# Last batch of a cross-covariance attention with a gated feed-forward: pairs of chunks, and every second block by seven products for eight

## The chip, the core and the metric

The kernel runs on one core of a Trainium2 chip. The core has five engines with instruction queues of their own, which meet only at semaphores: TensorE (PE in the profile) multiplies matrices into PSUM, VectorE (DVE) and ScalarE (ACT) read PSUM and SBUF, GpSimd (POOL) works on SBUF alone, and SyncE (SP) issues DMAs. [...] The metric is the device time of one execution in microseconds (us); lower is better. Before the change the median of three runs is 555.26 us (555.23 to 555.40).

## The reference

Four batches of 5824 tokens with 256 channels go through an attention over channels; its output goes as tokens through a feed-forward in which two products of the same input are multiplied with each other:

```python
qn = q / (norm(q, axis=1) + 1e-06);  kn = k / (norm(k, axis=1) + 1e-06)
a = softmax(kn.transpose(0, 2, 1) @ qn / tau)       # 256 x 256 per batch
x = (v @ a).reshape(B * S, D)                       # 23296 x 256
out = ((x @ w1) * (x @ w2)) @ w3 @ w_out            # 1024 hidden, 256 out
```

## The kernel before

Nothing non-linear stands between `v @ a` and `x @ w1`, so the kernel folds: for each batch `Wf = a @ [w1, w2]` (256 x 2 x 1024, bf16, by `fold`), and once `W_sb = w3 @ w_out` (1024 x 256). Per token what is left is `((v Wf1) * (v Wf2)) W_sb`. v comes in pieces of eight token groups by POOL's DMA queue and is transposed by DMA on SP's queue, into `vT` (channels on partitions).

A batch's tokens are cut into 12 chunks: eleven of 512 and a rest of 192. The loop at the end of the kernel goes over batches, chunks and the eight blocks j of 128 hidden columns; a step of it is a slot. In a slot `emit_ab` lets PE do four 512-column products: a = Wf1 block by vT (two, for the two channel halves, summed in PSUM) and b the same way with Wf2. ACT casts a to bf16 (`as`, line 663), and DVE multiplies it with b out of PSUM into `abh` in SBUF (line 676). The four PSUM banks `ab0` to `ab3` are taken in turn.

The second product, `abh` by `W_sb`, is done for whole chunks by a scheme of seven block products where the plain way has eight (`seven_products`): four operands S1 to S4, sums and differences of quarters of `abh` (lines 589 and 592, 128x1024 bf16 with both inputs in SBUF), then seven groups of eight 128-column products (`prodA`, `prodB`, `prodC`, line 570), with copies by ACT (`keep`, line 580) and additions by DVE (`join`, line 583) into the output tile. In batches 0 to 2 S1 to S4 are made by POOL, in the last batch by DVE. The groups wait in the list `pend` and are put behind the products of later slots, at most so many per slot as `room` allows. Chunks 10 and 11 of the last batch take the plain way (`emit_out`).

The program's order is written out by hand: what is emitted first stands first in its engine's queue. An agenda (`at`, `run_due`) puts the attention of batch n + 1 into batch n's slots by a running estimate of PE's time, and the loads of q, k and v, each behind a one-element copy on POOL (`gate`, line 645) that waits for a recent `abh`. In the last batch there is no next attention: what is left are the loads of v (pieces 2 to 5) and the feed-forward. SBUF tiles of 4 KB per partition (pieces, `abh` halves) share 21 buffers of the tag `big`.

Of the kernel before, what the change touches and what calls it, by code (L numbers as in the profile page):

```python
# [25 lines left out]
def kernel(  # L26
# [250 lines left out]
    def soft_units(n):  # L277
# [199 lines left out]
        if n == 0:  # L477
# [7 lines left out]
            + [(0.0, 11 + 1.4 * ct, lambda ct=ct: exps(ct)) for ct in range(CT)]  # L485
            + [(0.2, 15, sums)]
            + [(0.43, 16.5 + 1.1 * i, lambda i=i: fold(i)) for i in range(8)]
        )


    clock = [0.0]
    agenda = []
# [59 lines left out]
    def seven_products(b, c, k1, k2):  # L552
# [6 lines left out]
        w22 = [W_sb[:, 4 + j, P:] for j in range(4)]  # L559
        t1, t2, t3, t4 = ([T[:, i, j, :] for j in range(4)] for i in range(4))  # L560
        st, sums = {}, {}
        tags = {"A": "out0", "B": "out1", "C": "out1" if b < B - 1 else "out2"}
        adder = nc.gpsimd if b < B - 1 else nc.vector

        def product(nm, a, w, first=False):
            if first:
# [63 lines left out]
        def then(fn):  # L630
            return lambda: following.append(fn)

        if b == B - 1:
            return [S(1)], [
                [S(2), p1], [S(3), p5], [p6], [S(4), p7], [J("C", 1, 1), p2],
                [J("B", 0, 0), p4], [p3, J("C", 0, 1), store],
            ]
# [13 lines left out]
    def emit_ab(b, c, j):  # L651
        n = chunk_cols(c)
        tiles = []
        for w in range(2):
            t = psum.tile([P, 512], F32, name=f"{'ab'[w]}_{b}_{c}_{j}", **bank("ab"))
            for ct in range(CT):
                nc.tensor.matmul(  # L657
                    t[:, :n], lhsT=Wf[b][:, ct, w, j * P : (j + 1) * P], rhs=rhs_of(b, c, ct),
                    start=(ct == 0), stop=(ct == CT - 1),
                )  # L660
            tiles.append(t)
        a_sb = work.tile([P, 512], BF16, tag="a_sb", name=f"as_{b}_{c}_{j}", bufs=4)
        nc.scalar.copy(a_sb[:, :n], tiles[0][:, :n])  # L663
        if c == NCH - 1:
            if b % 2 == 0 and j == 0:
                lefts[b // 2] = work.tile([P, FT, 2, P + LEFT], BF16, tag="left", name=f"left_{b}", bufs=1)
            both = lefts[b // 2][:, j, b % 2, :]
            nc.vector.tensor_mul(both, a_sb[:, :n], tiles[1][:, :n])
            ab = both[:, :P] if b % 2 == 0 else both[:, LEFT:]
        else:  # L670
            if j == 0:
                halves[c] = [
                    in_pool.tile([P, 4, 512], BF16, tag="big", name=f"abh_{b}_{c}_{h}", bufs=BIG_BUFS) for h in range(2)
                ]
            ab = halves[c][j // 4][:, j % 4, :]
            nc.vector.tensor_mul(ab, a_sb, tiles[1])  # L676
        last_ab[0] = ab
        slot[0] += 1
        if not seven(b, c):
            if b == B - 1 or c == NCH - 1:  # L680
                lag = LAG if b == B - 1 else FT + LAG_FAST
                pend.append((slot[0] + lag, 1, lambda only=None: emit_out(b, c, j, ab, only)))
            elif j == FT - 1:
                for i in range(FT):
                    fn = lambda i=i, ab2=tuple(halves[c]): emit_half(b, c, i, ab2)
                    pend.append((slot[0] + 1 + LAG_FAST + i, 1, fn))
        elif j == FT - 1:
            sums, groups = seven_products(b, c, *halves[c])
            for i, fn in enumerate(sums):
                due_sums.append((slot[0] + 2 * i, fn))  # L690
            ready = slot[0] + 1 + (LAG_FAST if b < B - 1 else 0)
            for i, group in enumerate(groups):
                wait = 0 if b == B - 1 else i
                pend.append((ready + wait, 2, lambda group=group: [fn() for fn in group]))
        clock[0] += 4 * (n * MM_COL + MM_FIX)

    def emit_half(b, c, i, ab2):

# [267 lines left out]

    for b in range(B):
        make_agenda(b)
        order = [(c, j) for c in range(NCH) for j in range(FT)]
        if b == 0:  # L970
            order[: 2 * FT] = [(c, h * 4 + j) for h in range(2) for c in range(2) for j in range(4)]
        for s, (c, j) in enumerate(order):
            run_due()
            while following:
                following.pop(0)()
            scores_due(s)
            emit_ab(b, c, j)
# [51 lines left out]
```

## Time and profile before

| | |
|---|---|
| Median of three runs | 555.26 us |
| Profiled execution, first to last instruction (span) | 553.5 us; its time beyond the span is not listed |
| Granted TensorE clock, mean | 1.000 |
| PE, DVE, ACT, POOL busy | 98%, 79%, 68%, 55% |
| Last batch: first product of chunk 0 | 431.81 us from the span's start |
| Last batch: last matmul issued | about 549 us |
| POOL tensor operations after 434 us | four gate copies |

Busy time is what an engine's instructions cover, without the waits. Matmuls are pipelined, so their rows overlap: what one costs PE is the distance between starts. A row of the timeline has start, duration, engine, line, operation, output and inputs, and in brackets the idle time before it and what ended it. The chain of work follows the last instruction back to what released it, step by step; it says which engine sets the time.

### The profile page before, as it was taken

What the parts mean: (1) busy time and instruction counts of PE and PEld (TensorE: products, weight loads), DVE (VectorE), ACT (ScalarE), POOL (GpSimd) and SP (SyncE); (2) the same over time, 40 slices, a digit from 0 to 9 for tenths busy, and PEclk for the clock granted to TensorE, in tenths of its full rate; (3) what the DMA queues carried; (4) which work ended last, traced back from release to release, by engine and by line L of the source; (5) the groups of instructions that cost most, each with busy time, mean ns of one, the idle gap of its engine ahead of it and who ended that gap; (6) DMA issues with size and microseconds to landing.
All of it is one profiled execution on the core that took longest, in us unless ns stands there. A gap on an engine that the chain in (4) does not pass through costs nothing.

```text
span 553.5 us, 12330 instructions
## 1 busy us (share of the span) xinstructions
PE 542.1 (98%) x4630; PEld 352.9 (64%) x4630; DVE 435.5 (79%) x789; ACT 375.8 (68%) x757; POOL 304.8 (55%) x257
## 2 busy tenths in 40 slices
PE   7799999999999999999999999999999999999997
PEld 4564577766666666666667566666666666666665
DVE  5567747899976787988876788888877688988984
ACT  5436647788866777777766777777766666566663
POOL 4150022678889678889887588898987400010000
PEclk9999999999999999999999999999999999999999
DMA  9999888975666879576554777875650245343102
GB/s 213 211 206 209 167 164 201 224 180 82 152 140 155 191 150 165 126 147 136 128 127 122 153 153 156 164 147 124 147 115 40 83 117 117 91 110 82 77 40 97
DMA packets 74972, 77.61 MB, mean 140 GB/s; under 512 B 54176, under 2 KB 58784, under 8 KB 74912
## 3 DMA queue, kind: packets, MB, share of 16 engines
q0 software_dynamic: 15616, 38.93, 40.3%
q1 hardware_dynamic: 58928, 37.17, 24.2%
q8 instruction: 36, 0.59, 0.4%
q10 hardware_dynamic: 368, 0.72, 0.3%
q14 instruction: 24, 0.20, 0.1%
HBM read 78.91 MB, written 23.86 MB: 186 GB/s over the span
## 4 chain that ended last, share of the span: by engine, by line
PE 93%; DMA 5%; DVE 0%; ACT 0%; POOL 0%; issue 0%; POOLq 0%
PE a L657 28%; PE b L657 28%; PE prodA L570 13%; PE prodC L570 6%; PE G L200 5%; PE prodB L570 3%; DMA k<-in_k_dram 3%; PE o L707 3%; PE fold L428 2%; DMA q<-in_q_dram 2%; PE o_out L738 2%; PE w L882 1%; PE G L271 0%; PE narrow L452 0%; PE sqq L259 0%
## 5 line engine op out<-in xcount | busy, mean ns | idle before, releaser
L676 DVE TENSOR_TENSOR abh<-as,b 128x512 bf16<-128x512 bf16 x352 | 240.0, 684 | 82.0 <-ACT as L663 76.2
L663 ACT CAST as<-a 128x512 bf16<-128x512 f32 (+1 forms) x384 | 215.4, 562 | 94.8 <-PE a L657 61.5
L657 PE MATMUL a<-vT,Wf 128*128 128x512 bf16 x704 | 209.4, 379 | 0.1
L657 PE MATMUL b<-vT,Wf 128*128 128x512 bf16 x704 | 209.4, 379 | 0.0
L657 PEld LDWEIGHTS <-Wf 128*128 128x128 bf16 x1536 | 141.1, 98 | 100.6 <-issue 0.8
L570 PEld LDWEIGHTS <-S 128*128 128x128 bf16 x1248 | 82.6, 98 | 34.3
L212 DVE TENSOR_TENSOR acc<-acc,sq 128x512 f32<-128x512 f32 x132 | 91.6, 694 | 3.0 <-ACT sq L197 1.9
L580 ACT COPY osb<-prodA 128x256 f32<-128x256 f32 x156 | 58.1, 372 | 42.0 <-PE prodA L570 41.4
L589 POOL TENSOR_TENSOR S<-abh,abh 128x1024 bf16<-128x1024 bf16 x29 | 61.7, 2127 | 32.1 <-DVE abh L676 16.6
L570 PEld LDWEIGHTS <-abh 128*128 128x128 bf16 x936 | 62.0, 98 | 25.7 <-issue 0.2
L592 POOL TENSOR_TENSOR S<-S,abh 128x1024 bf16<-128x1024 bf16 x29 | 61.8, 2131 | 1.9
L592 POOL TENSOR_TENSOR S<-abh 128x1024 bf16<-128x1024 bf16 x29 | 61.8, 2131 | 0.1
L592 POOL TENSOR_TENSOR S<-abh,S 128x1024 bf16<-128x1024 bf16 x29 | 61.7, 2129 | 0.1
L645 POOL COPY gate_t<-abh 1x1 bf16<-1x1 bf16 x39 | 7.2, 185 | 80.1 <-DVE abh L676 79.9
L570 PE MATMUL prodA<-comb_T,S 128*128 128x128 bf16 x624 | 47.6, 219 | 0.0
L200 PE MATMUL G<-k,q 128*128 128x256 bf16 x276 | 47.0, 273 | 0.0
L197 ACT ACTIVATE sq<-q 128x512 f32<-128x512 bf16 x69 | 43.8, 634 | 0.0
L197 ACT ACTIVATE sq<-k 128x512 f32<-128x512 bf16 x69 | 43.4, 628 | 0.0
L583 DVE TENSOR_TENSOR osb<-prodC,osb 128x256 f32<-128x256 f32 x78 | 32.5, 417 | 0.0
L200 PEld LDWEIGHTS <-q 128*128 128x128 bf16 x276 | 23.9, 98 | 3.6
L570 PE MATMUL prodB<-W_sb,abh 128*128 128x128 bf16 x312 | 23.8, 219 | 0.1
L570 PE MATMUL prodC<-comb_T,S 128*128 128x128 bf16 x312 | 23.8, 219 | 0.0
(139 smaller groups left out, 444.0 us busy)
## 6 DMA issues: line engine op xcount, KB each, us to landing
out_dram<-osb SPq DMA_DIRECT2D x44, 512.0 KB, 3.2
k<-in_k_dram POOLq DMA_DIRECT2D x19, 512.0 KB, 8.3
v<-in_v_dram POOLq DMA_DIRECT2D x19, 512.0 KB, 5.2
q<-in_q_dram POOLq DMA_DIRECT2D x18, 512.0 KB, 5.8
w_wout<-in_moe_w_dram POOLq DMA_DIRECT2D x1, 2048.0 KB, 21.6
k<-in_k_dram POOLq DMA_DIRECT2D x4, 320.0 KB, 6.5
v<-in_v_dram POOLq DMA_DIRECT2D x4, 320.0 KB, 5.4
q<-in_q_dram POOLq DMA_DIRECT2D x3, 320.0 KB, 5.2
```

The costliest lines, as they stand in the source:

```text
L197: nc.scalar.activation(out=sqs[0][:, :, part, :], in_=src[:, o : o + 2, :], func=AF.Square)
L200: nc.tensor.matmul(G[:, ct, :], lhsT=qt[:, i, ct * P : (ct + 1) * P], rhs=kt[:, i, :], start=(pr == 0 and part == 0 and ct == 0), stop=(pr ...
L212: nc.vector.tensor_add(accs[n], accs[n], sqs[0][:, part - 2])
L570: nc.tensor.matmul(st[nm][:, i, :], lhsT=a[:, j, i * P : (i + 1) * P], rhs=w[j], start=(first and j == 0 and i == 0), stop=(j == 3), skip_ ...
L580: nc.scalar.copy(quarter(r, d), st["A"])
L583: nc.vector.tensor_add(quarter(r, d), st[nm], quarter(r, d))
L589: adder.tensor_add(x, a21, a22)
L592: adder.tensor_sub(x, u, w)
L657: nc.tensor.matmul(t[:, :n], lhsT=Wf[b][:, ct, w, j * P : (j + 1) * P], rhs=rhs_of(b, c, ct), start=(ct == 0), stop=(ct == CT - 1),)
L663: nc.scalar.copy(a_sb[:, :n], tiles[0][:, :n])
L676: nc.vector.tensor_mul(ab, a_sb, tiles[1])
L707: nc.tensor.matmul(t[:, k, :], lhsT=ab2[j // 4][:, j % 4, (2 * h + k) * P : (2 * h + k + 1) * P], rhs=W_sb[:, j, :], start=(j == 0 and k = ...
```

## The change

In the last batch, chunks 0 to 7 are taken in pairs (0, 1), (2, 3), (4, 5), (6, 7), and within a pair the blocks in twos. A period is one pair and two blocks: `jw` = 2k and `jn` = 2k + 1; there are 16 periods of four steps (`sub`). Block jn is computed plainly for both chunks (`plain`, eight 512-column products). Block jw, a and b for two chunks, is a 2 x 2 by 2 x 2 block product (two channel halves by two chunks, a and b by two channel halves), and is done by seven 512-column products where there were eight. It needs sums of weights (`weight_sum`, four DVE operations of 128x1024 per batch, before the batch begins) and sums of tokens (`token_sum`, four DVE operations of 128x512 per pair; those of the first pair in one go as the batch begins, the others one per period of the pair before). The running sum X stays in its bank through the period: it is copied to a second bank, Y, by ACT (PSUM to PSUM), and added on DVE to `t5`, a copy of the product T in SBUF, once into a third bank, Z, and once into a bf16 tile in SBUF, `b1`; further products are summed into X, Y and Z in place. Of the four factors, a1 times b1 is a DVE product of two SBUF tiles, and a0 times X the last DVE operation of the period.

The seven-product scheme of the output changes its order for chunks 0 to 7 of the last batch: operands at set slots and groups one per slot as in the batches before (`queue_products`, second chunk of a pair eight slots later), operands of chunks 0 to 6 on POOL, those of 7 to 9 on DVE. Chunks 8 and 9 keep the old order; `room` is 4 in the last batch outside of the pairs.

```diff
+            + [(0.0, 26.5 + 1.2 * i, lambda i=i: weight_sum(n, i)) for i in range(4) if n == B - 1]
...
+    PAIRED = {B - 1: (0, 2, 4, 6)}
...
+    def weight_sum(n, i):
+
+        if i == 0:
+            wsums[n] = [
+                in_pool.tile([P, 2, F], BF16, tag="big", name=f"wsum_{n}_{h}", bufs=BIG_BUFS) for h in range(2)
+            ]
+        s = [wsums[n][h][:, x, :] for h in range(2) for x in range(2)]
+        w = Wf[n]
+        if i == 0:
+            nc.vector.tensor_add(s[0], w[:, 0, 1, :], w[:, 1, 1, :])
+        elif i == 1:
+            nc.vector.tensor_sub(s[1], s[0], w[:, 0, 0, :])
+        elif i == 2:
+            nc.vector.tensor_sub(s[2], w[:, 0, 0, :], w[:, 0, 1, :])
+        else:
+            nc.vector.tensor_sub(s[3], w[:, 1, 0, :], s[1])
+
+    def token_sum(b, c, i):
+
+        if i == 0:
+            tsums[b, c] = in_pool.tile([P, 4, 4, P], BF16, tag="big", name=f"tsum_{b}_{c}", bufs=BIG_BUFS)
+        t = tsums[b, c]
+        b11, b12, b21, b22 = (rhs_of(b, c + d, ct) for ct in range(CT) for d in range(2))
+        if i == 0:
+            nc.vector.tensor_sub(t[:, 0], b12, b11)
+        elif i == 1:
+            nc.vector.tensor_sub(t[:, 1], b22, t[:, 0])
+        elif i == 2:
+            nc.vector.tensor_sub(t[:, 2], b22, b12)
+        else:
+            nc.vector.tensor_sub(t[:, 3], b21, t[:, 1])
...
+        late = b == B - 1 and c >= 2 + max(PAIRED[b])
...
-        adder = nc.gpsimd if b < B - 1 else nc.vector
+        adder = nc.vector if b == B - 1 and c > max(PAIRED[b]) else nc.gpsimd
...
-        if b == B - 1:
+        if late:
             return [S(1)], [
                 [S(2), p1], [S(3), p5], [p6], [S(4), p7], [J("C", 1, 1), p2],
                 [J("B", 0, 0), p4], [p3, J("C", 0, 1), store],
...
+    def queue_products(b, c, delay=0):
+
+        sums, groups = seven_products(b, c, *halves[c])
+        late = len(sums) == 1
+        if late:
+            pend.append((slot[0], 0, sums[0]))
+        for i, fn in enumerate(() if late else sums):
+            due_sums.append((slot[0] + delay + 2 * i, fn))
+        ready = slot[0] + delay + 1 + (0 if late else LAG_FAST)
+        for i, group in enumerate(groups):
+            pend.append((ready + (0 if late else i), 2, lambda group=group: [fn() for fn in group]))
...
+    def pair_begin(b, c, k):
+
+        x = periods[0] % 2
+        periods[0] += 1
+        st = pairs[b, c, k] = {"x": x}
+        st["X"] = psum.tile([P, 512], F32, name=f"X_{b}_{c}_{k}", tag=f"ab{x}", bufs=1)
+        j = slice(2 * k * P, (2 * k + 1) * P)
+        mm512(st["X"], Wf[b][:, 0, 0, j], rhs_of(b, c, 0), True)
+        st["Y"] = psum.tile([P, 512], F32, name=f"Y_{b}_{c}_{k}", tag="G", bufs=1)
+        nc.scalar.copy(st["Y"], st["X"])
...
+        if sub == 0:
+            st["T"] = psum.tile([P, 512], F32, name=f"T_{b}_{c}_{k}", tag="ab2", bufs=1)
+            mm512(st["T"], S[0][:, js], T[:, 0], True)
+            st["t5"] = work.tile([P, 512], F32, tag="sq", name=f"t5_{b}_{c}_{k}", bufs=2)
+            nc.scalar.copy(st["t5"], st["T"])
+            a = plain(b, c, jn, 0, "ab3")
+            st["a"] = cast(a, f"as_{b}_{c}_{jn}")
+        elif sub == 1:
+            mm512(X, S[1][:, js], T[:, 1], False)
+            st["Z"] = psum.tile([P, 512], F32, name=f"Z_{b}_{c}_{k}", tag="ab2", bufs=1)
+            nc.vector.tensor_add(st["Z"], X, st["t5"])
+            t = plain(b, c, jn, 1, f"ab{1 - st['x']}")
+            nc.vector.tensor_mul(ab(0, jn), st["a"], t)
+            last_ab[0] = ab(0, jn)
+            mm512(st["Y"], W[:, 1, 0, js], rhs_of(b, c, 1), False)
+            st["a0"] = cast(st["Y"], f"as_{b}_{c}_{jw}")
+        elif sub == 2:
+            a = plain(b, c + 1, jn, 0, "ab3")
+            st["a"] = cast(a, f"as_{b}_{c + 1}_{jn}")
+            mm512(X, S[2][:, js], T[:, 2], False)
+            st["b1"] = work.tile([P, 512], BF16, tag="b_sb", name=f"bs_{b}_{c + 1}_{jw}", bufs=1)
+            nc.vector.tensor_add(st["b1"], X, st["t5"])
+            mm512(st["Z"], S[3][:, js], rhs_of(b, c + 1, 1), False)
+            st["a1"] = cast(st["Z"], f"as_{b}_{c + 1}_{jw}")
+        else:
+            t = plain(b, c + 1, jn, 1, "G")
+            nc.vector.tensor_mul(ab(1, jn), st["a"], t)
+
+            def end():
+                mm512(X, W[:, 1, 1, js], T[:, 3], False)
+                nc.vector.tensor_mul(ab(1, jw), st["a1"], st["b1"])
+                if k < 3:
+                    pair_begin(b, c, k + 1)
+                elif c + 2 in PAIRED[b]:
+                    pair_begin(b, c + 2, 0)
+                nc.vector.tensor_mul(ab(0, jw), st["a0"], X)
+                last_ab[0] = ab(0, jw)
+                if k == 3:
+                    queue_products(b, c)
+                    queue_products(b, c + 1, FT)
...
+            if c in PAIRED.get(b, ()) and j == 0 and sub == [0] and c == 0:
+                for i in range(4):
+                    token_sum(b, c, i)
+            late = emit_pair(b, c, j, *sub) if sub else emit_ab(b, c, j)
+            if sub and c + 2 in PAIRED[b] and sub[0] == 3:
+                token_sum(b, c + 2, j)
...
-            room = 2
+            room = 4 if b == B - 1 and not sub else 2
...
+            for fn in late or ():
+                fn()
```

More of the change, by code (lines that the diff above doesn't have):

```diff
@@ L487, in soft_units @@
             + [(0.43, 16.5 + 1.1 * i, lambda i=i: fold(i)) for i in range(8)]
+            + [(0.0, 26.5 + 1.2 * i, lambda i=i: weight_sum(n, i)) for i in range(4) if n == B - 1]
         )
+    PAIRED = {B - 1: (0, 2, 4, 6)}
+    wsums = {}
+    tsums = {}
+    def weight_sum(n, i):
[26 more added lines that the diff above has]
+            nc.vector.tensor_sub(t[:, 3], b21, t[:, 1])
     clock = [0.0]
@@ L687, in emit_ab @@
         elif j == FT - 1:
[L688 to L694, printed above, removed]
-        clock[0] += 4 * (n * MM_COL + MM_FIX)
+            queue_products(b, c)
@@ new lines, with mm512 @@
+    pairs = {}
+    periods = [0]
+    def mm512(dst, lhsT, rhs, start):
+        nc.tensor.matmul(dst, lhsT=lhsT, rhs=rhs, start=start, stop=True, skip_group_check=True)
+        clock[0] += 4 * P * MM_COL + MM_FIX
+    def pair_begin(b, c, k):
[7 more added lines that the diff above has]
+        nc.scalar.copy(st["Y"], st["X"])
@@ new lines, in plain, with cast, emit_pair @@
+    def plain(b, c, j, w, tag):
+        t = psum.tile([P, 512], F32, name=f"{'ab'[w]}_{b}_{c}_{j}", tag=tag, bufs=1)
+        for ct in range(CT):
+            mm512(t, Wf[b][:, ct, w, j * P : (j + 1) * P], rhs_of(b, c, ct), ct == 0)
+        return t
+    def cast(t, name):
+        a_sb = work.tile([P, 512], BF16, tag="a_sb", name=name, bufs=4)
+        nc.scalar.copy(a_sb, t)
+        return a_sb
+    def emit_pair(b, c, k, sub):
+        W, T = Wf[b], tsums[b, c]
+        S = [wsums[b][h][:, x, :] for h in range(2) for x in range(2)]
+        jw, jn = 2 * k, 2 * k + 1
+        js = slice(jw * P, (jw + 1) * P)
+        if k == 0 and sub == 0:
+            for d in range(2):
+                halves[c + d] = [
+                    in_pool.tile([P, 4, 512], BF16, tag="big", name=f"abh_{b}_{c + d}_{h}", bufs=BIG_BUFS)
+                    for h in range(2)
+                ]
+        ab = lambda d, j: halves[c + d][j // 4][:, j % 4, :]
+        if (b, c, k) not in pairs:
+            pair_begin(b, c, k)
+        st = pairs[b, c, k]
+        X = st["X"]
+        late = []
+        if sub == 0:
[35 more added lines that the diff above has]
+                if k == 3:
+                    queue_products(b, c)
+                    queue_products(b, c + 1, FT)
+            late.append(end)
+        slot[0] += 1
+        return late
@@ L968 @@
         make_agenda(b)
-        order = [(c, j) for c in range(NCH) for j in range(FT)]
+        order = []
+        for c in range(NCH):
+            if c in PAIRED.get(b, ()):
+                order += [(c, k, sub) for k in range(4) for sub in range(4)]
+            elif c - 1 not in PAIRED.get(b, ()):
+                order += [(c, j) for j in range(FT)]
         if b == 0:
             order[: 2 * FT] = [(c, h * 4 + j) for h in range(2) for c in range(2) for j in range(4)]
-        for s, (c, j) in enumerate(order):
+        for s, (c, j, *sub) in enumerate(order):
             run_due()
@@ L976 @@
             scores_due(s)
-            emit_ab(b, c, j)
+            if c in PAIRED.get(b, ()) and j == 0 and sub == [0] and c == 0:
[4 more added lines that the diff above has]
+                token_sum(b, c + 2, j)
             lag = 0
```

## The prediction

> **What bounds the kernel now.** I read the page's busy line and its chain of work, then busy time by stage for the last batch, then the timelines of the engines there.
>
> ```profile
> PE 542.1 (98%) x4630; PEld 352.9 (64%) x4630; DVE 435.5 (79%) x789; ACT 375.8 (68%) x757; POOL 304.8 (55%) x257
> PE 93%; DMA 5%; DVE 0%; ACT 0%; POOL 0%; issue 0%; POOLq 0%
> 450.00:535.00 85.00, 85.00 (x761) 53.53 (x759) 74.36 (x130) 51.97 (x102) 2.94 (x7) 1.00 0.33 90
> ```
>
> The third line has PE, PEld, DVE, ACT and POOL busy in turn: in the last batch PE has no gap in 85 us at a granted clock of 1.00, DVE is busy 87%, POOL 3%. Every matmul taken away there is time won, and every wait put in front of PE is time lost.
>
> ```profile
> 500.73 0.59 PE L657 MATMUL b<-vT,Wf 128*128 128x512 bf16 x2
> 501.16 0.59 PE L657 MATMUL a<-vT,Wf 128*128 128x512 bf16 x2
> 501.59 0.59 PE L657 MATMUL b<-vT,Wf 128*128 128x512 bf16 x2
> 502.02 0.61 PE L570 MATMUL prodA<-W_sb,abh 128*128 128x128 bf16 x8
> 502.47 0.38 PE L657 MATMUL a<-vT,Wf 128*128 128x512 bf16 x1
> ```
>
> Starts 0.43 apart for two 512-column products: 0.215 each. A group of eight 128-column products: 0.45. One 512-column product is over 0.38 after its start.
>
> ```profile
> 501.79 0.58 ACT L663 CAST as<-a 128x512 bf16<-128x512 f32 x1 [0.28 <-PE a L657]
> 502.27 0.69 DVE L589 TENSOR_TENSOR S<-abh,abh 128x1024 bf16<-128x1024 bf16 x1
> 502.88 0.68 DVE L676 TENSOR_TENSOR abh<-as,b 128x512 bf16<-128x512 bf16 x1
> 503.47 0.68 DVE L592 TENSOR_TENSOR S<-S,abh 128x1024 bf16<-128x1024 bf16 x1
> L548 DVE TENSOR_TENSOR comb_T<-W_sb x1: 418/418/418, 82.7 to 82.7; 128x512 bf16<-128x512 bf16 x1
> ```
>
> The cast starts 0.42 after the start of the product that it waits for (501.16 + 0.215), so an engine picks up 0.04 after an end. Back to back, DVE starts a 0.69 operation every 0.60, an overlap of about 0.08. The last line (the tile's own view) is the only 128x512 bf16 operation with both inputs in SBUF: 0.42, so 0.34 back to back.
>
> ```profile
> 494.64 0.68 DVE L592 TENSOR_TENSOR S<-abh 128x1024 bf16<-128x1024 bf16 x1
> 494.85 0.51 POOL L645 COPY gate_t<-abh 1x1 bf16<-1x1 bf16 x1 [17.26 <-DVE abh L676]
> L645 POOL COPY gate_t<-abh x39: 176/176/510, 72.3 to 494.9; 1x1 bf16<-1x1 bf16 x39
> 427.70 2.12 POOL L592 TENSOR_TENSOR S<-S,abh 128x1024 bf16<-128x1024 bf16 x1
> 429.78 2.12 POOL L592 TENSOR_TENSOR S<-abh 128x1024 bf16<-128x1024 bf16 x1
> 431.86 2.13 POOL L592 TENSOR_TENSOR S<-abh,S 128x1024 bf16<-128x1024 bf16 x1
> ```
>
> This is the suspicious place. The one-element gate copy on POOL has a median of 0.176; its longest, 0.51, began inside a DVE operation with two SBUF inputs and ended 0.04 after it (495.36 against 495.32). An S operand takes POOL 2.12. In the trace of before POOL's S operands and such two-input DVE operations never run side by side: batches 0 to 2 put them all on POOL, the last on DVE.
>
> **The change part by part.** Removed: one of sixteen 512-column products per period (two chunks, two blocks), 16 periods: 16 x 0.215 = 3.44 off PE.
>
> Per period PE now issues T, a, a | X, b, b, Y | a, a, X, Z | b, b | X, next X; a bar is a place where one product group may follow. DVE does the Z sum, a product, the b1 sum, a product, a token sum, the product of a1 and b1, and last the product of a0 and X. The sums with PSUM are as the accumulator's row (L212, 0.69). Work per period: PE 15 x 0.215 + 3.5 x 0.45 = 4.80; DVE 5 x 0.60 + 2 x 0.34 + 1.5 joins x 0.34 = 4.19; ACT six copies of 0.58 and two keeps of 0.37 = 4.22. None takes PE's place by its sum. A PSUM-to-PSUM copy of 128x512 has no row; between the 128x256 keep (0.37) and the fold's 0.69 I take the cast's 0.58, its size. Even at 0.69 X would start by 1.15 of the period, and b waits longer for the loop below.
>
> The new wait that matters: the first b goes into the bank that held the previous period's X, which DVE's last product reads. From the start of that period's last b matmul: 0.42 to the product on DVE, 0.60, token sum 0.34, a1 with b1 0.34, the last product 0.69, 0.04 back: 2.43. PE needs from there b, X, next X, T, a, a, X: 7 x 0.215 = 1.51, plus product groups after b and after a: 2.41 with both, 1.96 with one, 1.51 with none. So 0.02, 0.47 or 0.92 of wait per boundary. The PE order of the changed kernel shows which: periods 2 and 3 hold only single 128x256 products of chunk 11 (0.11 each), periods 4 and 5 nothing, since products of chunk 0 wait for its pair and for slow S operands. Boundaries 1-2: 0.36; 2-3: 0.70; 3-4: 0.81; 4-5: 0.92; 5-6: 0.47; seven more at 0.02: 0.14; the last three have no token sum: 0. Sum 3.40. Those products come later, two a slot, at no PE cost.
>
> Start: the four weight sums (0.69 each) sit between the multiplications of chunk 11, the token sums behind them. Walked through the DVE rows from 428.85, the first token sum ends at 433.67; T would be ready at 432.03. Wait 1.68 with the 0.04. End: chunk 9's sums still run on DVE, with fewer slots before their products: from the order about 0.50 for S2, 0.15 for S3, and 0.10 for chunk 8: 0.75. Loads of v stand behind S operands on POOL, up to 8.5 us late; the last three are needed 15 us or more after they are issued and land in 5.2. SP's stores and transposes follow by as much, with the same room.
>
> Without anything else: -3.44 + 3.40 + 1.68 + 0.75 = +2.39, 557.65.
>
> **The port hold.** The change puts chunks 0 to 6's S operands on POOL, 2.12 each, eight per pair, while DVE does token sums, a1 x b1 and the weight sums, all with two SBUF inputs. The gate row shows POOL kept off by such an operation; whether DVE is kept off by POOL no row shows. Bounds: nothing, or the whole 2.12 for each DVE operation that meets POOL. These are 8 each in the pairs of chunks 2 and 4 and 4 in chunk 6's pair: at most 20 x 2.12 = 42. As the gate row has the second comer wait to the very end, I take the symmetric case: when POOL is busy, half an operand on average (1.06). POOL works 8 x 2.08 (its spacing) = 16.7 per pair; a pair is four periods of about 4.85 plus the waits, some 25 us, so POOL is busy 0.67 of it. Token sum: 0.67 x 1.06 = 0.71; a1 x b1 right behind it: a whole operand if POOL gets in between, which I take in half of the cases, 0.67 x 2.12 / 2 = 0.71. So 1.42 a period on a loop without slack, x 8 = 11.4. In chunk 6's pair, without token sums, about 0.78 x 1.06 = 0.83 less 0.34 of slack, x 4 = 2.0. At the start weight sum, S3, weight sum, S4 and weight sum alternate, the first token sum ends at 437.45, and T waits 5.46 in place of 1.68: +3.8. Sum 17.2: 555.26 - 3.44 + 3.40 + 1.68 + 0.75 + 17.2 = 574.8. With one hold a period and half the rest: 5.7 + 1.0 + 1.9 = 8.6, 566.2. With two half operands a period whatever POOL's share (2.12): 17.0 + 2.8 + 3.8 = 23.6, 581.2.
>
> [...]
>
> The sum stands on the profiled execution: span 553.5, with the median of the runs (555.26) 1.7 above it for what lies around; I add the difference to the median.
>
> **The rivals.** (1) No hold of DVE by POOL, only the waits: 557.65. For it: a single row, and in the direction that costs nothing. Against: that POOL waited out a whole DVE operation. (2) The saving shows, the other side: if DVE's loop from b to b is not 2.43 but 1.6 or less, PE never waits at a boundary, and with the weight sums out of T's way the time goes towards 555.26 - 3.44 = 551.8; with the end's 0.75 552.6. It decides when all waits together stay under 2.3. For it: DVE has 0.6 a period to spare by its sum. Against: the loop is a chain of waits, each with a row. (3) ACT or DVE as the bound by throughput: 4.22 and 4.19 against 4.80, 16 periods at most 0; dropped. That PE issues 16 products fewer is in its order, so the change does what it says.
>
> **How the numbers follow.** Hold 0.66 (566 to 581, middle 574.8), waits only 0.22 (556 to 559), saving shows 0.12 (551.8 to 554.5). The forecast is the hold's. Range 554.5 to 587: below lies most of the 0.12, above about 0.05 for more full holds. A measurement tells 0.2% (1.1 us) from no change: slower, the hold and most of the waits, 0.82; within, 0.06; faster 0.12. The hold's own range is 566 to 581.
>
> **What would show it.** Hold: DVE's 128x512 two-input operations in the pairs of chunks 2 to 6 spread from 0.42 to over 2, or idle for a POOL end, PE idle before b for DVE, POOL's S often over 2.13, POOL and DVE never in two-input work together. Waits only: those rows stay at 0.42, PE idles in the first five boundaries (0.4 to 0.9 each) and before T. Saving: PE without gaps and 3.4 shorter. The hold is wrong if a token sum inside an S operand takes 0.42. The price is wrong if POOL has no S ready when the token sum ends (less), or each operation meets a fresh one (more).

## The result

The changed kernel takes 595.04 us (median of four runs, 592.88 to 597.85); the kernel before takes 555.25 us. The ratio is 1.072, with a 95% interval of 1.068 to 1.0759. The profiled execution took 592.88 us, with a span of 591.1 us against 553.5.

The page of the changed kernel, the lines that answer to the first ones shown of before: busy times, the clock in 40 slices, and the chain by engine.

```profile
PE 550.8 (93%) x4614; PEld 355.0 (60%) x4614; DVE 466.5 (79%) x813; ACT 387.5 (66%) x789; POOL 365.7 (62%) x285
...
PEclk9999999999999999999999999999989789999999
...
PE 82%; DVE 7%; DMA 4%; issue 4%; ACT 2%; POOL 0%; DVEq 0%; ACTq 0%; POOLq 0%
```

TensorE issues 16 products fewer, as the change says (4614 against 4630), and yet is busy 8.7 us longer; the digits below 9 in the clock's row say most of it: for 17.1 us of the last batch it ran at a granted clock of 0.50. DVE, at 0% of the chain before, has 7% of it.

The same stretch of the last batch as was shown of before (columns: length, then busy time and count of PE, PEld, DVE, ACT and POOL, then granted clock, DMA share and GB/s), and the waits of TensorE with their totals, counts and longest:

```profile
450.00:535.00 85.00, 61.93 (x447) 35.27 (x445) 73.02 (x95) 43.61 (x92) 49.66 (x29) 0.92 0.28 63
```

```profile
PE b L745 <- DVE abh L824: 22.9, 12, 5.3
...
PE T L745 <- DVE tsum L520: 2.6, 1, 2.6
PE prodC L608 <- DVE osb L621: 1.7, 2, 0.9
```

PE had no gap in these 85 us; now 23 us of them are gaps, the clock is 0.92, and POOL is busy 50 us where it was busy 3. The first b of a period waits for the last product (L824), as the prediction's loop says, but for up to 5.3 us. Here is that longest wait, in the timelines of DVE, POOL and PE:

```profile
478.00 5.52 DVE L524 TENSOR_TENSOR tsum<-vT 128x512 bf16<-128x512 bf16 x1
483.44 0.41 DVE L819 TENSOR_TENSOR abh<-as,bs 128x512 bf16<-128x512 bf16 x1
483.78 0.67 DVE L824 TENSOR_TENSOR abh<-as,X 128x512 bf16<-128x512 bf16 x1
```

```profile
476.37 0.57 POOL L120 DMA_DIRECT2D v<-in_v_dram  x1 [0.31 <-ACT as L768]
476.96 2.14 POOL L630 TENSOR_TENSOR S<-S,abh 128x1024 bf16<-128x1024 bf16 x1
479.04 2.12 POOL L630 TENSOR_TENSOR S<-abh 128x1024 bf16<-128x1024 bf16 x1
481.12 2.11 POOL L630 TENSOR_TENSOR S<-abh,S 128x1024 bf16<-128x1024 bf16 x1
```

```profile
478.79 0.38 PE L745 MATMUL X<-tsum,wsum 128*128 128x512 bf16 x1
484.51 1.01 PE L745 MATMUL b<-vT,Wf 128*128 128x512 bf16 x2 [5.34 <-DVE abh L824]
485.31 0.63 PE L745 MATMUL Y<-vT,Wf 128*128 128x512 bf16 x1
485.74 1.06 PE L608 MATMUL prodB<-W_sb,abh 128*128 128x128 bf16 x8
486.59 1.04 PE L745 MATMUL a<-vT,Wf 128*128 128x512 bf16 x2
```

A token sum, 0.42 us of work, is begun at 478.00 while S2 is on POOL and ends at 483.52, 0.29 after the end of S4 (483.23): it stood through the rest of S2, all of S3 and all of S4. Behind it come a1 x b1, the last product and the b that waits. The row of the token sum shows no wait ahead of it; the time stands in the operation itself. And from 484.5 the products are twice as far apart as before (a group of eight 0.85 us, not 0.45). The clock over that stretch, from the same view as above:

```profile
484.50:487.00 2.50, 2.49 (x12) 1.41 (x12) 1.69 (x4) 0.59 (x1) 0.00 (x0) 0.50 0.53 175
```

**Where the 37.6 us of span come from.** The trace counts a wait from the modelled end of the last product, 0.16 us after the next one could have started (a 512-column product shows 0.38 us, the spacing is 0.215), so each wait costs 0.16 more than it lists. Added up over PE's starts in the last batch: waits 32.3 us (about 22 listed in the periods beside POOL's operands, 4.2 at the start, 1.3 at the boundaries that POOL does not touch, 1.6 at the end, the rest the 0.16 of each), slow clock 7.3, gaps too short to be listed 1.5 more than before, products saved 3.4: 32.3 + 7.3 + 1.5 - 3.4 = 37.7. The trace's record of the granted clock has TensorE at half speed for 17.1 us of the last batch (3.41, 6.83, 3.41 and 3.41), so that the clock can have cost 8.5 us at most.

The theory after this result: an operand on POOL and a DVE operation with both inputs in SBUF hold each other off, as forecast, but DVE can be passed over several times in a row (at two ends in the lines above), and the idleness slows TensorE's clock on top. "Port", in the forecast and the expectations, is my name for whatever the two cannot have at once; the traces show the holds and not what lies behind them. Rivals: POOL's work costs whatever runs beside it; DVE is late for reasons of its own (its operations, their order); the start and the products' order cost without any hold.

### The profile page after: what moved, and what is told of

The parts are those of the page before. It is cut to its first block, busy times and chain, and to the rows that moved or that the text cites. A ratio compares the mean times of both kernels' runs of the same rounds, so it can differ in the third digit from the quotient of the medians.

```text
span 591.1 us, 12398 instructions
## 1 busy us (share of the span) xinstructions
PE 550.8 (93%) x4614; PEld 355.0 (60%) x4614; DVE 466.5 (79%) x813; ACT 387.5 (66%) x789; POOL 365.7 (62%) x285
## 3 DMA queue, kind: packets, MB, share of 16 engines
q0 software_dynamic: 15616, 38.93, 37.6%
q1 hardware_dynamic: 58928, 37.17, 22.7%
## 4 chain that ended last, share of the span: by engine, by line
PE 82%; DVE 7%; DMA 4%; issue 4%; ACT 2%; POOL 0%; DVEq 0%; ACTq 0%; POOLq 0%
PE a L695 22%; PE b L695 22%; PE prodA L608 11%; PE G L200 5%; PE prodC L608 5%; PE prodB L608 3%; DMA k<-in_k_dram 3%; PE b L745 2%; PE o L844 2%; PE fold L428 2%; DMA q<-in_q_dram 2%; PE a L745 2%; PE o_out L875 1%; DVE abh L819 1%; DVE abh L824 1%
## 5 line engine op out<-in xcount | busy, mean ns | idle before, releaser
L714 DVE TENSOR_TENSOR abh<-as,b 128x512 bf16<-128x512 bf16 x288 | 196.3, 684 | 72.9 <-ACT as L701 68.0
L701 ACT CAST as<-a 128x512 bf16<-128x512 f32 (+1 forms) x320 | 178.2, 558 | 73.7 <-PE a L695 54.0
L695 PE MATMUL a<-vT,Wf 128*128 128x512 bf16 x576 | 171.3, 379 | 0.1
L695 PE MATMUL b<-vT,Wf 128*128 128x512 bf16 x576 | 171.3, 379 | 0.0
L695 PEld LDWEIGHTS <-Wf 128*128 128x128 bf16 x1280 | 118.2, 98 | 83.8 <-issue 0.6
L627 POOL TENSOR_TENSOR S<-abh,abh 128x1024 bf16<-128x1024 bf16 x36 | 76.6, 2128 | 69.3 <-DVE abh L824 30.2
L630 POOL TENSOR_TENSOR S<-S,abh 128x1024 bf16<-128x1024 bf16 x36 | 76.8, 2133 | 2.4
L630 POOL TENSOR_TENSOR S<-abh,S 128x1024 bf16<-128x1024 bf16 x36 | 77.7, 2159 | 0.1
L630 POOL TENSOR_TENSOR S<-abh 128x1024 bf16<-128x1024 bf16 x36 | 77.7, 2159 | 0.1
L745 PE MATMUL b<-vT,Wf 128*128 128x512 bf16 x64 | 20.6, 406 | 22.9 <-DVE abh L824 22.9
L745 PEld LDWEIGHTS <-Wf 128*128 128x128 bf16 x176 | 16.6, 102 | 41.9 <-issue 33.1
L621 DVE TENSOR_TENSOR osb<-prodC,osb 128x256 f32<-128x256 f32 x78 | 32.5, 417 | 0.0
L768 ACT CAST as<-Y 128x512 bf16<-128x512 f32 x16 | 9.4, 586 | 29.4 <-PE Y L745 29.4
```

The lines of the kernel that those rows point to most:

```text
L621: nc.vector.tensor_add(quarter(r, d), st[nm], quarter(r, d))
L627: adder.tensor_add(x, a21, a22)
L630: adder.tensor_sub(x, u, w)
L695: nc.tensor.matmul(t[:, :n], lhsT=Wf[b][:, ct, w, j * P : (j + 1) * P], rhs=rhs_of(b, c, ct), start=(ct == 0), stop=(ct == CT - 1),)
L745: nc.tensor.matmul(dst, lhsT=lhsT, rhs=rhs, start=start, stop=True, skip_group_check=True)
```

## Experiments

### Without GpSimd's operands in the last batch

```
         def operand(i):
+            if b == B - 1 and c <= max(PAIRED[b]):
+                sums[i] = {1: a21, 2: a11, 3: a21, 4: a12}[i]
+                return
             x = sums[i] = work.tile(...)
```

> Leaves out the operands S1 to S4 of chunks 0 to 6 in the last batch (the products read quarters of abh in their place), so POOL does no tensor work while the pairs run; all else stands. Port theory (DVE's two-input operations are held by POOL's, and PE's clock falls after the long waits): in the pairs of chunks 2, 4 and 6 PE idles 23 us before b and loses some 8 us to the slow clock; both go: 562 (559 to 565), token sums and a1 x b1 all at 0.42, the start as before. Late-operand theory (PE or DVE wait for POOL's results through semaphores): also about 562. Slow-operation theory (token sums or a1 x b1 are slow in themselves): stays above 585.

Measured: 564.95 us, ratio 1.0174 (1.0145 to 1.0204). The three groups of TensorE's waits shown above are now these (the last product has line 827 here):

```profile
PE T L748 <- DVE tsum L520: 2.6, 1, 2.6
PE prodC L608 <- DVE osb L621: 1.7, 2, 0.9
PE b L748 <- DVE abh L827: 1.1, 5, 0.2
```

30.1 us of the loss go with POOL's operands: 22.9 us of waits for the last product become 1.1, and every token sum and a1 x b1 in the pairs takes 0.41 to 0.42. The start is untouched, since the operands that stand beside it are those of the batch before.

### POOL's operands kept, DVE's two-input operations taken away

Later pairs read the first pair's token sums, and a1 is multiplied with X, from PSUM, in place of b1:

```
     def token_sum(b, c, i):
+        if c > 0:
+            tsums[b, c] = tsums[b, 0]
+            return
...
-                nc.vector.tensor_mul(ab(1, jw), st["a1"], st["b1"])
+                nc.vector.tensor_mul(ab(1, jw), st["a1"], X)
```

> POOL keeps its operands; on DVE no operation with two SBUF inputs is left in the pairs of chunks 2 to 6: the token sums of these pairs are left out (all pairs use the first pair's) and a1 is multiplied with X out of PSUM in place of b1. Port theory: 562 (559 to 565), with POOL's S operands at 2.12 next to it. Late-operand theory: POOL works as before, so above 585. Slow-operation theory: 562. Only the port theory has both this run and the one without POOL's work at 562.

Measured: 563.91 us, 1.0156 (1.0126 to 1.0185). In the same 85 us:

```profile
450.00:535.00 85.00, 83.92 (x701) 50.18 (x700) 72.56 (x124) 61.15 (x128) 61.39 (x35) 1.00 0.34 85
```

POOL is busier than in the changed kernel (61.4 against 49.7 us) and costs nothing: PE 83.92 busy, clock 1.00. DVE's operations are fewer here, but without POOL's operands all of them stood, at 0.41 to 0.42 each. So it is neither POOL's work nor late operands nor DVE's own work, but POOL's meeting with DVE's operations that have both inputs in SBUF.

### Only the token sums taken away

The first half of the edit above, with a1 x b1 left as it was.

> Only the token sums of the later pairs are left out; a1 x b1 keeps its two SBUF inputs. Port theory: a1 x b1 comes first at the port and takes over most of the wait that the token sum had: 575 to 592. Slow-operation theory with the token sums as culprit (strided inputs): about 565. Late-operand theory: above 585.

Measured: 582.77 us, 1.0495 (1.0465 to 1.0526). From the waits of TensorE and the timeline of DVE in this kernel:

```profile
PE b L748 <- DVE abh L827: 15.0, 8, 4.7
```

```profile
471.25 5.53 DVE L822 TENSOR_TENSOR abh<-as,bs 128x512 bf16<-128x512 bf16 x1
```

Line 822 is a1 x b1. In the changed kernel's pairs of chunks 2 and 4 it took 2.33 us at most; with the token sums gone it takes their place, with the same 5.5 us. So it is not the token sum as such: what the two share is that they need both inputs from SBUF when POOL is in a row of operands. Taking away 8 of the 20 such operations saved 12 us of the 31 that taking all away saves.

### The operands on DVE

```
-        adder = nc.vector if b == B - 1 and c > max(PAIRED[b]) else nc.gpsimd
+        adder = nc.vector if b == B - 1 else nc.gpsimd
```

> All operands S1 to S4 of the last batch on DVE, as before the change, everything else as changed: the sum of DVE's work per period goes from 4.19 to 5.39 us against PE's 4.80, so in 12 periods some 0.55 each: port theory 562 + 6 = 568 (563 to 573), DVE without holds, busy over 95% in the pairs, waits of PE below 1.5 us each and the clock at 1.00 there. Late-operand theory: 560 to 565.

Measured: 570.22 us, 1.0269 (1.024 to 1.0299). No hold is left (22 token sums and a1 x b1 at 0.42 on average), and this version, which leaves nothing out, takes back 25 of the 40 us. It stays behind the first two, and DVE is now the fuller engine: 82.67 of the same 85 us, with PE at 82.02. By the starts, TensorE's waits and short gaps in the last batch come to 16.4 us where the version without POOL's operands has 11.5; that DVE's fullness makes the difference is read from this, not tested.

### Each operand in two halves

```
-                adder.tensor_add(x, a21, a22)
+                for xs, us, ws in zip(pieces_of(x), pieces_of(a21), pieces_of(a22)):
+                    adder.tensor_add(xs, us, ws)
```

and the same for the differences; pieces_of cuts a tile in two for the last batch.

> The change with each running sum of the last batch made by two GpSimd instructions of half the size, back to back, instead of one; nothing is left out. If VectorE gets in at the end of whatever GpSimd instruction is running (the term of my forecast, at most one operand for each operation), the holds are halved, to 1.1 us at most, and the time falls to about 575 (568 to 582). If VectorE gets in only where GpSimd itself has to wait or is out of work (holds through a whole series), the halves change nothing: 595 us (589 to 601), with holds of 4 to 5 us still there.

Measured: 597.08 us, 1.0739 (1.0712 to 1.0766); no gain. The longest hold, from DVE's and POOL's timelines:

```profile
473.09 5.95 DVE L524 TENSOR_TENSOR tsum<-vT 128x512 bf16<-128x512 bf16 x1
```

```profile
472.06 2.27 POOL L634 TENSOR_TENSOR S<-S,abh 128x512 bf16<-128x512 bf16 x2
474.28 2.25 POOL L634 TENSOR_TENSOR S<-abh 128x512 bf16<-128x512 bf16 x2
476.50 2.25 POOL L634 TENSOR_TENSOR S<-abh,S 128x512 bf16<-128x512 bf16 x2
```

The token sum stands from 473.09 to 479.04, past five ends of a POOL instruction, and gets in after the last. My "at most one operand for each operation" is gone. But "only when POOL has to wait" is not the whole rule either: four token sums that met S1 here took 1.25 us, not 2.21 to 2.26 as in the changed kernel, so they did get in between two halves that follow each other directly. In the changed kernel, too, a token sum begun at 460.02 got in at the end of S2 (461.55), with S3 lengthened to 2.29 us by it. These are the lines of that case:

```profile
460.02 1.81 DVE L520 TENSOR_TENSOR tsum<-vT 128x512 bf16<-128x512 bf16 x1
```

```profile
459.43 2.12 POOL L630 TENSOR_TENSOR S<-S,abh 128x1024 bf16<-128x1024 bf16 x1
461.51 2.29 POOL L630 TENSOR_TENSOR S<-abh 128x1024 bf16<-128x1024 bf16 x1
```

Both long holds of the changed kernel (5.52 and 4.41), and the longest here, are of rows that POOL did right after a load's DMA issue (476.37 in the lines of the result). That goes for every one in the changed kernel, the one without token sums and this one: all seven holds past the end of an operand stand in such rows, and in rows without an issue ahead 22 of 22 held operations got in at the first end. But not every operation in a row behind an issue loses: in the changed kernel one begun at 537.16 got in at the end of S3. What decides which of the two goes on at an instruction's end stays open.

The issues held DVE as well. In this kernel one a1 x b1, 0.42 us of work, met two of them with no operand running and took 1.36:

```profile
526.01 1.36 DVE L823 TENSOR_TENSOR abh<-as,bs 128x512 bf16<-128x512 bf16 x1
```

```profile
525.85 0.55 POOL L117 DMA_DIRECT2D v<-in_v_dram  x1
526.39 0.56 POOL L120 DMA_DIRECT2D v<-in_v_dram  x1
```

It ended at 527.37, 0.42 after the second issue, and the operand behind the issues began at 526.97.

### GpSimd paced, two-input operations behind the product that frees the bank

```
+            if b == B - 1 and adder is nc.gpsimd and i % 2 == 1:
+                gate()
...
+                nc.vector.tensor_mul(ab(0, jw), st["a0"], X)
                 nc.vector.tensor_mul(ab(1, jw), st["a1"], st["b1"])
+                last_ab[0] = ab(1, jw)
+                if c + 2 in PAIRED[b]:
+                    token_sum(b, c + 2, k)
+                    last_ab[0] = tsums[b, c + 2][:, k, 0, :]
                 if k < 3:
                     pair_begin(b, c, k + 1)
                 elif c + 2 in PAIRED[b]:
                     pair_begin(b, c + 2, 0)
-                nc.vector.tensor_mul(ab(0, jw), st["a0"], X)
-                last_ab[0] = ab(0, jw)
```

The token sum is no longer called beside the last slot's b. Nothing is left out.

> The change with two things altered. GpSimd gets its running sums S1, S2 and S3, S4 two at a time, each two behind a one-element copy that waits for VectorE's last operation of a period; and on VectorE the two operations with both inputs in SBUF (a1 times b1, and the token sum) stand behind the product that frees the bank, and not ahead of it. Nothing is left out. GpSimd's work (4.24 us in a period of 4.85) then starts when VectorE's two-input operations are over, and what still overlaps has 1.5 us of cover behind it. Port theory: the waits of b for the last product fall from 22.9 + 1.8 us to under 3, the slow stretches of the middle go with them, and what is left is the start (4.2 us of waits and about 2 of slow clock), the end (1.6) and the saving of 3.44: 560 us (556 to 566). If it were GpSimd's work in itself that costs, whatever its place: about 590.

Measured: 567.83 us, 1.0226 (1.0208 to 1.0243), 27 us better than the change, 1.8 above the top of what I expected. The largest wait in the middle and its cause, from PE's waits and DVE's timeline:

```profile
PE X L747 <- DVE Z L801: 3.7, 6, 1.0
```

```profile
491.08 2.04 DVE L822 TENSOR_TENSOR abh<-as,bs 128x512 bf16<-128x512 bf16 x1
493.05 0.41 DVE L524 TENSOR_TENSOR tsum<-vT 128x512 bf16<-128x512 bf16 x1
```

a1 x b1 still meets the end of POOL's pair of operands (0.9 to 2.2 us each time): what is behind it, the Z sum, is late in place of the product. There is no room: a chunk pair without holds lasts about 19.4 us, POOL's eight operands take 17.0 of it and DVE's eight two-input operations 8 x 0.42 = 3.4, together more than there is; by their spacings back to back (2.08 and 0.34) they would just fill it. That no order can keep the two apart is argued from this, not shown: two orders were tried.

### The pairs from chunk 2 on

The paced version with PAIRED = {B - 1: (2, 4, 6)}, weight sums in the last four slots of chunk 0, first token sums in the last two of chunk 1; GpSimd is paced from chunk 1 on, and `room` is 4 only from chunk 8 on.

> The paced version, with the pairs starting at chunk 2 instead of chunk 0: six chunks by seven products, so 12 products less than before and not 16 (-2.58 us), and the weight sums and first token sums in slots of chunks 0 and 1 in which GpSimd has nothing. If the start's waits (4.2 us and about 2 of slow clock) come from VectorE being late through GpSimd's hold, they go: 555 us (551 to 559), that is -2.58, +1.6 at the end, and up to 2 of small waits. If the start costs as much wherever it stands: 560 or more.

Measured: 564.19 us, 1.0158 (1.0143 to 1.0173), a miss. The start's waits are gone, but the first token sum met an operand of chunk 0 (1.99 us), T waited 1.96 us for it, and the clock fell behind it (0.55 on average from 452.60 to 455.90); the Z waits stay (2.6 us).

### a1 straight from PSUM

Against the version just told: a1 x b1 reads a1 from its bank (one input in SBUF, and no cast), the token sum stands behind the last product, the weight sums and first token sums are in slots 2 to 6 of chunk 0, and chunk 7's operands are on GpSimd. The second kernel has the same with the pairs from chunk 0 on and the start of the change.

```
-            st["a1"] = cast(st["Z"], f"as_{b}_{c + 1}_{jw}")
...
+            nc.vector.tensor_mul(ab(1, jw), st["Z"], st["b1"])
             t = plain(b, c + 1, jn, 1, "G")
             nc.vector.tensor_mul(ab(1, jn), st["a"], t)
```

> The pairs start at chunk 2 (-2.58 us), and three things are altered against the change: a1 times b1 reads a1 straight from its PSUM bank (one input in SBUF, no cast for it), so that the token sums are VectorE's only two-input operations; each token sum stands behind the last product of its period, and GpSimd's operands follow it two at a time; weight sums and first token sums stand in chunk 0, where GpSimd is idle; chunk 7's operands stay on GpSimd. Nothing is left out. The port then has 17.0 us of operands and 1.6 us of token sums to hold in a chunk pair of some 19.4 us, where the change has 17.0 and 3.3. Port theory: waits for VectorE in the pairs under 1.5 us in sum, no slow stretch, the start's wait of 1.96 us gone, the end's 1.6 left or part of it: 554.5 us (552.5 to 558), level with the kernel before or a little under it. If the pairs cost through anything else (ScalarE, the copies within PSUM, weight loads): 560 or more.

> The same kernel with the pairs from chunk 0 on, as in the change, and its weight sums and first token sums where the change has them. The difference to its neighbour is the start: 4.2 us of waits and some 2 of slow clock against 0.86 more saved. 560.5 us (557 to 564).

Measured: 561.21 us, 1.0108 (1.0093 to 1.0123), and with the pairs from chunk 0 on 567.11 us, 1.0215 (1.0198 to 1.0232). They miss by 6.7 and 6.6 us, and the first falls where I had said beforehand that the pairs cost through something else than the port (560 or more). The pairs of the first, by the view of busy times, and what TensorE waits for in its last batch:

```profile
451.00:533.00 82.00, 80.08 (x656) 47.25 (x654) 68.60 (x120) 52.18 (x107) 63.99 (x50) 1.00 0.35 88
```

```profile
PE prodC L607 <- DVE osb L620: 0.9, 1, 0.9
PE X L746 <- ACT Y L758: 0.9, 2, 0.4
PE b L696 <- DVE abh L715: 0.8, 2, 0.4
PE prodA L607 <- ACT osb L617: 0.5, 1, 0.5
PE T L746 <- DVE abh L814: 0.4, 2, 0.2
...
```

The port theory's part is as expected: with POOL busy 64 of 82 us the clock is 1.00 and the waits for DVE in the pairs are 0.6 us (0.9 with the first T's). What is left is hardly the hold. By the starts, 11 listed waits cost 6.0 us with their drains, gaps too short to be listed another 2.4 more than before; less 2.6 us of saved products that is the 5.8 us by which its span (559.3) is longer than before. My expectation counted only the listed waits of the pairs and of the end, without the 0.16 us that each costs besides and without the short gaps. What makes the short gaps was not tried. This is the fastest version tried that leaves nothing out, and it is slower than the kernel before by 1.1%; none beat it.

### The start

The version without GpSimd's operands, and now also without weight sums and first token sums:

```
     def weight_sum(n, i):
+        if n == B - 1:
+            return
...
     def token_sum(b, c, i):
+        if c == 0:
+            tsums[b, c] = Plain(b, c)
+            return
```

where Plain hands out the tokens themselves, and the products read the weights themselves.

> The version without GpSimd's operands in the last batch, and now also without the four weight sums and the first four token sums (the products read unsummed weights and tokens in their place, so the output of these blocks is wrong; the other token sums stay). Left of GpSimd's work beside the last batch are the operands of the batch before. If the start's waits come from VectorE standing before these eight sums, held by those operands, the 2.57 us for the token sum, the 1.63 us for the joins and the slow stretch behind them (about 2) go: 564.95 - 6.2 = 558.7 us (557 to 560.5). If the start costs through the order of TensorE's work itself, 563 to 565.

Measured: 558.39 us, 1.0059 (1.0039 to 1.0078). The waits of T and of the joins are gone; 564.95 - 558.39 = 6.6 us is what the eight sums at the start cost, clock included. What remains, 3.2 us above the kernel before, is by the starts 3.4 us saved against 6.8 of waits, drains and small gaps, at the boundaries and the end.

### What slows the clock

The kernel before, with waits for TensorE put into its last batch: ahead of one b product VectorE fills its bank a few times.

```
+            if b == B - 1 and w == 1 and j == 4 and 1 <= c <= 7:
+                for _ in range((0, 2, 3, 4, 5, 6, 7, 9)[c]):
+                    nc.vector.memset(t, 0.0)
             for ct in range(CT):
                 nc.tensor.matmul(t[:, :n], ...)
```

> The kernel before, with a wait for TensorE put into seven chunks of the last batch, some 14 us apart: ahead of one b product, VectorE fills its bank 2, 3, 4, 5, 6, 7 and 9 times (the products overwrite it). No port is held. By the trace of the changed kernel, waits of up to 2.8 us leave the speed of the products alone, and from 3.4 us on they run at half speed for 3 to 5 us. Taking 0.5 to 0.6 us for one filling: seven waits of about 1 to 5 us, in sum some 18 to 22 us, and three slow stretches of about 2 us lost each, 580 us (573 to 588). If the slow stretches of the changed kernel came from anything but idleness, there are none here, and the time is 555 plus the waits alone.

In the second kernel it is always three fillings, in chunks 0 to 7 at slots 4, 6, 1, 4, 7, 2, 5 and 0.

> The kernel before with eight waits of the same length (three fillings of the bank by VectorE, which gave 2.61 us) at different places of chunks 0 to 7. In the earlier run a wait of 3.28 us left TensorE at full speed and one of 3.34 us halved it, but the changed kernel was slow after 2.57 us and the paced one after 1.96, so length alone is in doubt. If only the length decides and the limit is near 3.3 us, none of the eight is followed by slow products: 8 times 2.7 us, 577 us (575 to 579). If it also counts where the wait falls (in something like a fixed stretch of time), some of the eight are followed by a stretch at half speed and others not, each stretch losing 1.5 to 2 us: 579 to 588.

Measured: 591.07 us (1.0643, 1.0608 to 1.0678) and 580.33 us (1.0454, 1.0429 to 1.0479). The first is above what I expected, since its waits are longer: 1.68 to 6.61 us, 27.4 listed in sum. In both, GpSimd has no operand in the last batch (in the first it is busy 305.1 us in all, 304.8 in the kernel before), and the mean clock is 0.977 and 0.994 where the kernel before has 0.998 to 1.000: waits alone were enough to slow it. But it is not the length of the wait that decides. From PE's timeline of the first, after a wait of 3.28 us and one of 3.34:

```profile
473.91 0.59 PE L660 MATMUL b<-vT,Wf 128*128 128x512 bf16 x2 [3.28 <-DVE b L658]
474.34 0.61 PE L570 MATMUL prodA<-comb_T,S 128*128 128x128 bf16 x8
474.79 0.59 PE L660 MATMUL a<-vT,Wf 128*128 128x512 bf16 x2
...
487.89 0.59 PE L660 MATMUL b<-vT,Wf 128*128 128x512 bf16 x2 [3.34 <-DVE b L658]
488.32 0.61 PE L570 MATMUL prodA<-comb_T,S 128*128 128x128 bf16 x8
488.77 0.72 PE L660 MATMUL a<-vT,Wf 128*128 128x512 bf16 x2
489.28 1.06 PE L660 MATMUL b<-vT,Wf 128*128 128x512 bf16 x2
490.13 1.06 PE L570 MATMUL prodB<-W_sb,abh 128*128 128x128 bf16 x8
```

and of the second, after two equal waits:

```profile
495.07 0.59 PE L660 MATMUL b<-vT,Wf 128*128 128x512 bf16 x2 [2.34 <-DVE b L658]
495.50 0.61 PE L570 MATMUL prodC<-W_sb,S 128*128 128x128 bf16 x8
...
518.24 1.01 PE L660 MATMUL b<-vT,Wf 128*128 128x512 bf16 x2 [2.34 <-DVE b L658]
519.05 1.06 PE L570 MATMUL prodA<-comb_T,abh 128*128 128x128 bf16 x8
```

The slow products are those with a second column of 1.0 us instead of 0.6. After the 3.34 us they begin only 1.2 us behind the wait; of the two equal waits one is followed by them and one is not. By the trace's record of the granted clock, the slow stretches of the first run end at 492.52, 509.59, 526.66 and 547.14: 17.07, 17.07 and 20.48 apart, that is 5, 5 and 6 times 3.41. In the changed kernel they end at 439.7, 470.4, 487.5 and 518.2, which is 9, 5 and 9 such steps; in the second clock kernel 23 steps apart. The slow stretches of the changed kernel are 3.41, 6.83, 3.41 and 3.41 long, whole steps again. So in these runs the clock changes on a grid of 3.41 us. That it goes by the idleness of the stretch before is my reading, and the next table is what it rests on. Laid on that grid (its place taken from the record in each run), the idle share of a stretch (by the starts: the part in which no product was streaming, 0.215 us for 512 columns, twice that at half speed) sorts all of those in the last batch:

| Run | Idle share of the stretch, next one slow | Idle share, next one at full speed (largest) |
|---|---|---|
| changed kernel | 0.81, 0.71, 1.00, 0.82 | 0.61, 0.60, 0.49 |
| waits of rising length | 0.64, 0.80, 0.78, 0.68 | 0.55, 0.54, 0.47 |
| eight waits of three fillings | 0.74, 0.67 | 0.59, 0.57, 0.55 |
| pairs from chunk 2 on | 0.62 | 0.30 |
| only the token sums taken away | 0.62, 0.86, 0.70 | 0.52, 0.51, 0.47 |
| operands in two halves | 0.81, 0.81, 0.79, 0.66 | 0.55, 0.55, 0.48 |
| one input from PSUM (no slow stretch) | | 0.58, 0.51, 0.33 |

The remaining traces agree: at the start, 0.67 to 0.81 ahead of the one slow stretch that four of them have, and 0.53 at most ahead of full speed.

Once slow, it stayed slow in these runs behind stretches with an idle share of 0.31 and more, and came back behind those with 0.20 and less. The length of a wait does not sort them: products were slow behind waits of 1.96 us (pairs from chunk 2 on), 2.34 (one of the two above) and 2.57 (T in the changed kernel), and not behind the 3.28 above. The idle share of a stretch does, and nothing in these kernels chooses where a wait falls in it. This may be why the changed kernel's own runs lie 5 us apart (592.9 at a mean clock of 0.985, 597.9 at 0.977): the lower mean is some 9 us more at half speed, which can cost up to 4.6. Why the one run had more of it than the other was not tried.

## Why the prediction was right and wrong

- The forecast's mechanism holds: DVE's 128x512 two-input operations spread from 0.42 to 5.52 us, b waits for the last product, and taking away either side of the meeting takes away 30 to 31 us (564.95 and 563.91 against 595.04). That DVE waits too, and to the very end, was inferred from the one gate row, in which POOL waits; the runs show both directions. In the changed kernel's last batch ten token sums and a1 x b1 began while an operand ran, and each ended 0.27 to 0.29 us after an operand's end; where DVE went on first, the operand behind took up to 2.31 us in place of 2.12. So the two engines do not meet only at semaphores, as the description of the core has it.
- **The step that failed is the price of one hold**: 2.12 as the most that one operation can lose, and 0.71 on average for a token sum and for a1 x b1. It took it for certain that DVE gets in at the end of a POOL operand. The rows of the changed kernel sum to 22.7 us of holds over the same 20 operations (1.14 each, not 0.71), and 9.1 of them are two token sums that were passed over at one or more ends in a row (5.52 and 4.41). The two, let in at the first end, would have cost 3.2, and the sum 16.8: near the 13.4 forecast for the pairs. The sum's own bound, 42, was not reached; it was the bound for one operation that fell.
- **A term was missing altogether: the clock.** I let every wait cost its length. 7.3 us of the 37.6 are products at half speed after waits; without them the time would have been 587.7, still just above the top of the range (587), which was built from waits alone. The page of before, at a clock of 1.00 throughout, could not show it.
- Term by term, in us of the span:

| Term | Forecast | Changed kernel |
|---|---|---|
| Products saved | -3.4 | -3.4 |
| Waits beside POOL's operands, in the pairs | 13.4 | 23.3 |
| Waits at the start | 5.5 | 4.7 |
| Boundaries without a hold | 3.4 | 2.3 |
| The end | 0.75 | 2.1 |
| Slow clock | none | 7.3 |
| Gaps too short to be listed | none | 1.5 |
| Sum | 19.6 | 37.7 |

- The start: forecast 5.46 of wait for T, weight sums held by the batch before. Without POOL's operands 6.6 us hang on the eight sums there, of which 2.6 is the wait for T, 1.6 are joins (L621) queued behind the held weight sums on DVE, that I had not counted, and about 1.7 the slow clock behind them. Right in cause and nearly in size, in other places than said.
- The boundaries without a hold: forecast 3.40, with 0.92 at most. Without POOL's operands seven are listed, of 0.16 to 0.27 each, 1.5 in sum and 2.7 with drains; near in sum, wrong in shape.
- The end: forecast 0.75, listed 1.6 (0.87 of it a product group that waits for a join).
- Rival 1, waits only (557.65), has the version without POOL's operands and without the start's sums nearest to it. Without the 1.68 of the start my sum for that version is 555.97; it took 558.39, so that the small terms were 2.4 us short, 0.8 of it at the end, the rest drains and gaps. Rival 2 (the saving shows) fell everywhere: the 2.6 to 3.4 us are lost again in a dozen or so small waits. Throughput of ACT or DVE was no bound in the change; DVE came near to one only with the operands on it (82.67 of 85 us).

## What to carry to other kernels

Before moving work onto GpSimd beside a VectorE that has operations with both inputs in SBUF, add up both engines' time on such work in the stage: where the sum exceeds the stage (17.0 + 3.4 against 19.4 us here), expect them to wait for each other, as they did in both orders tried, and one hold can last over several GpSimd instructions (5.52 us over three here), so price it by the length of GpSimd's row of work, not by one instruction. Let VectorE read one of the inputs from PSUM where that is possible: with a1 x X so read and no token sums in the later pairs, the time was 563.91 us in place of 595.04, and that operation took 0.68 to 0.69 us inside a running operand (begun at 458.52 there, the operand from 457.99 to 460.11). And where TensorE runs without a gap, an estimate from the table above: count waits of 2.1 us or more that can fall together in one stretch (0.62 of 3.41, the lowest idle share with a slow stretch behind it) as their length and up to 1.7 us on top (half of 3.41) for each stretch at half speed.

## What the hardware showed that I had not expected

- VectorE can be passed over at several ends of GpSimd instructions in a row: 5.52 us for a 0.42 us operation, past two ends; with halves 5.95 us, past five. In rows without an issue ahead it got in at the first end (22 of 22). A load's DMA issues on GpSimd take part: in the changed kernel one a1 x b1 stood for 3.32 us (529.93 to 533.25), beginning among two of them (0.55 and 0.56) and ending behind an S1; in the version with halves one stood through two with no operand beside it (1.36 us).
- In these runs TensorE's granted clock went to 0.50 for whole stretches of 3.41 us, each time behind a stretch of which 0.62 or more was idle; behind 0.61 (changed kernel) it stayed at full speed. The two lie about as close as shares worked out from the starts can be told apart (some 0.01).
- A copy from PSUM to PSUM is hardly cheaper than one into SBUF: Y<-X 0.57 us on ScalarE (L757), the cast of the same size 0.59.
